# A row ring of twice the size, x loads behind four transposes, index operations behind the low halves, in a routed expert kernel on one core

## The chip, the cores and the metric

One Trainium2 chip, one core of it, one launch. The metric is the device time of the kernel in microseconds (us), lower is better.

## The reference

The input is x of 8 x 3584 tokens with 192 features. A causal filter of 7 taps per head (8 heads of 24 features, taps by a softmax over the weight row) gives 28672 mixed tokens. Each token goes to one of 8 experts:

```
logits = normalize(x) @ normalize(emb).T / tau
e      = argmax(logits);  gate = softmax(logits)[e]
out[t] = gate * (relu(x[t] @ w1[e]) @ w2[e])     # 192 -> 1024 -> 192
```

All of it is float32.

## The kernel before, in words

**Stages.** Tokens are handled in 16 chunks of 1792 (112 partitions x 16). `mix` filters a chunk by matmuls (`conv`, L423) and takes square norms. `route` scales the chunk (`scaled`, L480 and L482) and splits every number into a high and a low float16 half (`rest`, L489 to L495), four groups of four tiles. For each group `turn` (L686) has SP issue a DMA transpose of the rows from SBUF into `xtb`, and `logits` (L676) multiplies it by the embeddings. `rank` picks the expert and counts a place in its list. `put` and `scatter` (L692) have POOL write each token's row, with its number and gate, into the expert's list `rows_d` in DRAM by an indirect DMA, 16 per chunk. `load_x` (L402, L411) loads the x of two chunks later into the buffer that this chunk leaves.

**Experts.** After some chunks `hand_out` opens a phase: each expert gets a block of the next 128 to 512 rows of its list. `fetch` gives SP the loads of one block: two DMA transposes from `rows_d` (L821) into a buffer `e_xT` and one small load `e_mt` (L870) of numbers and gates. Before the change there are three `e_xT` buffers, and `expert` fetches so that the block about to start and the two after it have their loads in SP's queue; a load waits for the scatters that it needs and for its buffer. `block` then runs. For each of its hidden tiles five matmuls go into PSUM (`h_ps`, L940), ACT writes the high halves (relu, L944) and DVE the low halves (L946). Then `gate` has DVE clip the token numbers (`id`, `masked`, L852) and scale the gates (`g`, L915); `id` and `g` have three buffers each. Last come 24 matmuls per 128 rows into `o_ps` (L961), ACT's `y` scaled by `g` (L966), and POOL's indirect DMA of `y` to the rows `id` of the output (L968).

**What sets the order.** SP runs its queue exactly as the program emits it. On PE, ACT, DVE and POOL the framework orders the instructions by a simulated timeline, within the dependences that it knows; an instruction that looks ready there may stand ahead of others that were emitted before it. A dependence without a semaphore only fixes the order on an engine. In `run`, a planner with its own clock (`self.clock`, in us of TensorE work) interleaves pieces of `route`, `mix` and `rank` with the steps of the blocks; logits are emitted at least 7.0 of it after the last transpose (`TURN`). At the end `last_blocks` adds 8 blocks of 512 rows and 20 small ones whose expert is known only at run time; for these, DVE copies the weights into `slot` (L809, L813), the last 6146 columns of the tile `work`. Nothing else uses `slot` after the weights have been prepared.

Of the kernel before, what the change touches and what calls it, by code (L numbers as in the profile page):

```python
# [12 lines left out]
F16 = mybir.dt.float16  # L13
F32 = mybir.dt.float32
# [3 lines left out]
ALU = mybir.AluOpType  # L18
# [4 lines left out]
H = 8  # L23
# [7 lines left out]
NT = 16  # L31
# [12 lines left out]
NFC = F // 128  # L44
# [6 lines left out]
GX = 4  # L51
# [19 lines left out]
AHEAD = 0.4  # L71
OUT = 1.9, 1.6
COST = 14.4, 12.6
WAIT = 0.5, 0.5
# [16 lines left out]
class _Sub:  # L91
    def __init__(self, T, u, need, e=None, c=None, sel=None, j=None):
        self.T, self.u, self.need = T, u, need
        self.e, self.c, self.sel, self.j = e, c, sel, j
        self.xT = self.mt = None


class _Moe:
    def __init__(self, ctx, tc, x, weight, emb, tau, w1, w2, out):
        self.tc, self.nc = tc, tc.nc  # L100
        self.x, self.weight, self.emb, self.tau = x, weight, emb, tau
        self.w1, self.w2, self.out = w1, w2, out
        B, S, _ = x.shape
        self.B, self.S, self.N = B, S, B * S
        self.nch = self.N // CT
        self.per_b = S // CT
        self.cap = self.N + PAD
        self.dummy = E * self.cap
        pool = lambda name, bufs, **k: ctx.enter_context(
            tc.tile_pool(name=name, bufs=bufs, **k))  # L110
        self.cp = pool("const", 1)
        self.xp = pool("xload", 2)
        self.sp = pool("small", 2)
        self.lp = pool("lone", 1)
        self.ep = pool("expert", 3)
        self.yp = pool("y", 3)
        self.op = pool("out", 4)
        self.mp = pool("meta", 6)
        self.hp = pool("phase", 6)
        self.rings = {k: pool("ps_" + k, n, space=PSUM)  # L120
                      for k, n in (("r", 1), ("l", 1), ("h", 6))}

        self.res = self.cp.tile([128, E * RES], F16, name="res")
        self.work = self.cp.tile([128, 2 * NFC * 512 + S2 + RES - W2], F16, name="work")
        self.hid = self.work[:, 0:2 * NFC * 512]
        self.slot = self.work[:, 2 * NFC * 512:]
        self.xtb = self.cp.tile([128, NT // GX, XW], F16, name="xtb")
        self.rows2 = self.cp.tile([TP, 2, NT, SW], I32, name="rows2")
        self.ids = self.cp.tile([TP, NT], I32, name="ids")
        self.xtn = 0  # L130
        self.wexp = self.cp.tile([128, E, 2], I32, name="wexp")
        self.si = self.cp.tile([128, E, 2], I32, name="w_si")
        self.ws = self.cp.tile([128, E, 2], I32, name="w_s")
        self.acc = self.cp.tile([128, E, 2], F32, name="w_acc")
        self.g0 = self.cp.tile([128, E], F32, name="g0")
        self.dp = pool("scratch", 1, space=DRAM)
        self.rows_d = self.dp.tile([E * self.cap + PAD * NJ, RW], I32, name="rows_d")
        self.scatters, self.pend, self.step = [], [], None
        self.nput, self.final = 0, False
        self.vacant = [0.0, 0.0]  # L140
        self.lims, self.pace = {}, 1.0
        self.xts, self.mixed, self.n2 = [], {}, {}
        self.raw = {}
        self.tiles, self.lgs, self.ranks, self.zs = {}, {}, {}, {}
        self.subs, self.ready, self.at, self.copied = [], 0, 0, 0
        self.clock, self.mm = 0.0, None
# [51 lines left out]
    def constants(self):  # L198
        nc, cp = self.nc, self.cp
        nc.gpsimd.memset(self.xtb[:].rearrange(  # L200
            "p h (a k t) -> p (h a) k t", k=4, t=TP)[:, :, 3, 0:HALO], 0.0)
        nc.gpsimd.memset(self.rows2[:, :, :, XD + 2:], 0)
        nc.gpsimd.iota(self.ids, pattern=[[TP, NT]], base=TP - 1,
                       channel_multiplier=-1)
        head = self.ep.tile([128, 4 * 512], F16, tag="xT", name="head")[:].bitcast(F32)
        self.idf, self.onef = head[:, 0:128], head[:, 128:256]
        make_identity(nc, self.idf)
        self.idh = head[:, 256:320].bitcast(F16)
        nc.vector.tensor_copy(out=self.idh, in_=self.idf)
        nc.gpsimd.memset(self.onef, 1.0)  # L210
        self.oneh = cp.tile([128, 128], F16, name="oneh")
        nc.gpsimd.memset(self.oneh, 1.0)

        self.lth = cp.tile([128, 128], F16, name="lth")
        nc.gpsimd.memset(self.lth, 1.0)
        nc.gpsimd.affine_select(
            out=self.lth, in_=self.lth, pattern=[[1, 128]], base=0,
            channel_multiplier=-1, compare_op=ALU.is_gt, fill=0.0)

        tmp = self.op.tile([128, D], F32, tag="y", name="tmp")[:, 0:2 * E + 64].bitcast(I32)  # L220
        e8i = tmp[0:TP, 0:E]
        nc.gpsimd.iota(e8i, pattern=[[-1, E]], base=E, channel_multiplier=0)
        self.e8 = cp.tile([TP, E], F32, name="e8")
        nc.vector.tensor_copy(out=self.e8, in_=e8i)

        self.rst = cp.tile([TP, E, NT], F32, name="rst")
        nc.gpsimd.memset(self.rst, 1.0)
        nc.gpsimd.memset(self.rst[:, :, 0:1], 0.0)

        rn = tmp[:, E:E + NJ]  # L230
        nc.gpsimd.iota(rn, pattern=[[128, NJ]], base=1, channel_multiplier=1)
        self.rn = cp.tile([128, NJ], F32, name="rn")
        nc.vector.tensor_single_scalar(out=self.rn, in_=rn, scalar=float(self.N),
                                       op=ALU.mult)

        cbi = tmp[:, E + 64:]
        nc.gpsimd.iota(cbi, pattern=[[self.cap, E]], base=0, channel_multiplier=0)
        self.cb = cp.tile([128, E], F32, name="cb")
        nc.vector.tensor_copy(out=self.cb, in_=cbi)

        self.start = cp.tile([128, E], F32, name="start")
        nc.vector.tensor_copy(out=self.start, in_=cbi)

    def conv_taps(self, w):
# [10 lines left out]
        nc.vector.tensor_scalar(out=w, in0=w, scalar1=z[:, 0:1], scalar2=None,  # L255
                                op0=ALU.mult)

        seq = self.ep.tile([128, 3 * 512], F16, tag="xT", name="cseq")[
            0:H, :].bitcast(F32)[:, 0:2 * 128]
        nc.vector.memset(seq, 0.0)  # L260
        nc.vector.tensor_copy(out=seq[:, TP + 9:TP + 9 + KT], in_=w)
        sd = self.dp.tile([H, 2 * 128], F32, name="cseq_d")
# [235 lines left out]
    def route(self, c):  # L498
        xTs = []
# [3 lines left out]
        for g in range(NT // GX):  # L503
            self.scaled(c, g)
            yield 0.9, 0.85
            self.rest(c, g)
            yield 0.95, 0.0
            if g < 2:
                xTs.append(self.turn(c, g))
        if c + 2 < self.nch:  # L510
            self.load_x(c + 2)
        for g in range(2, NT // GX):
            xTs.append(self.turn(c, g))
        yield self.clock + TURN
        for g in range(NT // GX):
            self.logits(lg, xTs[g], g)
# [174 lines left out]
    def scatter(self, idx, src):  # L691
# [5 lines left out]
            self.tc.declare_no_dep(i, group=k, reason="rows are distinct")  # L697
        self.tc.add_to_no_dep_group("put", i)
        self.scatters.append(i)


    def pads(self):
# [130 lines left out]
    def first_rows(self, k):  # L833
        nc = self.nc
        if not k:
# [3 lines left out]
                tensor=m.tensor, offset=m.offset,  # L839
                ap=[[RW, 128], [RW * self.cap, E], [1, 2]])).ins], NT)  # L840
            self.x0 = []
        x = self.ep.tile([128, 4 * 512], F16, tag="xT", name="e_xT")
        for i in range(4):
            e = 4 * k + i
            v = x[:, i * 512:(i + 1) * 512].rearrange("p (k t) -> p k t", t=128)
            self.after(self.rows_of(e * self.cap, v, 128, NT), NT)
            self.x0.append(v)

    def masked(self, ids, lim, name):
        n = int(np.prod(ids.shape[1:]))  # L850
        o = self.yp.tile([128, 8], I32, tag="id", name=name)[:, 0:n]
        self.nc.vector.scalar_tensor_tensor(  # L852
            out=o, in0=ids, scalar=float(self.N), in1=lim, op0=ALU.min, op1=ALU.max)
        return o

    def fetch(self):
        nc = self.nc
# [3 lines left out]
        if s.u == 0:  # L861
# [1 line left out]
            self.row = nc.sync.value_load(at, min_val=0, max_val=E * self.cap)  # L863
        row = self.row + s.u if s.u else self.row
        T = s.T
        s.xT = self.ep.tile([128, 4 * 512], F16, tag="xT", name="e_xT")[
            :, 0:4 * T].rearrange("p (k t) -> p k t", t=T)
        lds = self.rows_of(row, s.xT, T, s.need)
        s.mt = self.mp.tile([128, 4, 2], I32, tag="mt", name="e_mt")[:, 0:T // 128]
        lds.append(nc.sync.dma_start(  # L870
# [23 lines left out]

    def expert(self):
        nc = self.nc
        while self.ready < min(self.at + 3, len(self.subs)):
            self.fetch()
        s = self.subs[self.at]
        self.copy_w1(self.at)  # L900
# [7 lines left out]
        def gate():  # L908
            if s.e is None:
                ids.extend(s.mt[:, a, 0:1] for a in range(nj))  # L910
            else:
                a = s.u // 128
                m = self.masked(s.mt[:, :, 0], self.lims[s.c][0][:, s.e, a:a + nj], "id")
                ids.extend(m[:, a:a + 1] for a in range(nj))
            nc.vector.tensor_scalar(  # L915
                out=g[:, 0:nj], in0=s.mt[:, :, 1].bitcast(F32),
# [4 lines left out]
    def block(self, T, e, xT, ids, g, gate=None):  # L921
# [12 lines left out]
        for b in range(0, NFC, m):  # L934
            ps = self.ps("h", [128, m, T], F32, "h_ps")
            for c in range(m):
# [6 lines left out]
            self.mm = mm.ins.name  # L943
            self.step = nc.scalar.activation(  # L944
                out=hh[:, b:b + m, :], in_=ps, func=AF.Relu).ins
            nc.vector.scalar_tensor_tensor(  # L946
                out=hl[:, b:b + m, :], in0=ps, scalar=0.0, in1=hh[:, b:b + m, :],
                op0=ALU.max, op1=ALU.subtract)
            self.dt = 5 * m * T / 2400
            yield self.slack(m * T)  # L950
        if gate:
# [213 lines left out]
```

## Time and profile before

| | us |
|---|---|
| median of 3 runs | 1276.82 (1273.12 to 1283.05) |
| profiled execution | 1275.99 |
| its span, first to last instruction | 1274.0 |

| engine | busy us | share of the span |
|---|---|---|
| PE matmul | 1130.4 | 89% |
| DVE | 668.7 | 52% |
| ACT | 599.7 | 47% |
| POOL | 511.8 | 40% |

The mean granted TensorE clock is 0.96. The DMA queue of SP took 37.7% of the 16 DMA engines' span, that of POOL 14.0%. Busy shares are averages over a head of about 100 us (weights and first chunks), a long middle in which chunks are routed beside the experts, up to about 945 us, and a tail of experts alone. "Idle before, releaser" in the profile names what ended an engine's idle time; a wait for several semaphores is put down to the one that came last.

### The profile page before, as it was taken

Reading aid. Unit: us, or ns where it says so; the run is one execution under the profiler, and the core shown is the slowest. Engines: PE = TensorE matmul, PEld = TensorE weight load, DVE = VectorE, ACT = ScalarE, POOL = GpSimd, SP = SyncE. Lnnn points to the kernel's source line nnn. Section 1 sums busy time; section 2 is a strip of 40 time slices with the busy share of each in tenths; the row PEclk is TensorE's granted clock in tenths of the full one; section 3 lists DMA queues with packets and bytes.
Section 4 is the critical chain, followed back from the end, with each engine's and each line's share of the span. In section 5 each row is a group of like instructions: output and inputs, shape, how many; then the busy total and the mean of one; then the engine's idle time right before and its main releaser. Section 6 shows DMA issues by size and latency. Waiting matters only on the chain. (4 is left out here: it accounts for less than half of the span.)

```text
span 1274.0 us, 29634 instructions
## 1 busy us (share of the span) xinstructions
PE 1130.4 (89%) x11188; PEld 905.9 (71%) x11188; DVE 668.7 (52%) x1939; ACT 599.7 (47%) x1414; POOL 511.8 (40%) x523
## 2 busy tenths in 40 slices
PE   5667998787798999898999989999889999999997
PEld 3466887686677877676667666778668778877776
DVE  5996463574374563736364627554643334445443
ACT  4974454454365365454545445643334433333333
POOL 1336225545355447362625343554742213222222
PEclk8878999998998999899999999999999999999999
DMA  9747547756767839475656655574422212322220
GB/s 259 202 112 201 124 82 178 169 117 132 159 121 171 163 85 220 85 172 105 144 118 135 130 117 98 104 143 80 107 74 57 58 45 55 55 52 51 51 49 24
DMA packets 324777, 146.64 MB, mean 115 GB/s; under 512 B 266590, under 2 KB 315101, under 8 KB 324624
## 3 DMA queue, kind: packets, MB, share of 16 engines
q1 hardware_dynamic: 300960, 93.98, 37.7%
q0 software_dynamic: 23664, 50.68, 14.0%
q8 instruction: 89, 1.46, 0.5%
q14 instruction: 64, 0.52, 0.1%
HBM read 38.35 MB, written 51.05 MB: 70 GB/s over the span
## 5 line engine op out<-in xcount | busy, mean ns | idle before, releaser
L961 PEld LDWEIGHTS <-work 128*128 128x128 f16 x5472 | 462.8, 99 | 83.7 <-DVE work L946 36.8
L940 PE MATMUL h_ps<-e_xT,res 128*128 128x384 f16 (+3 forms) x3520 | 493.9, 295 | 28.4 <-DVE work L946 14.2
L961 PE MATMUL o_ps<-res,work 128*128 128x192 f16 x4992 | 458.5, 249 | 41.7 <-DVE work L946 36.8
L940 PEld LDWEIGHTS <-res 128*128 128x128 f16 x3520 | 308.4, 99 | 185.4 <-issue 45.0
L946 DVE SCALAR_TENSOR_TENSOR work<-h_ps,work 128x384 f16<-128x384 f32 (+1 forms) x536 | 316.7, 605 | 170.0 <-ACT work L944 167.2
L944 ACT ACTIVATE work<-h_ps 128x384 f16<-128x384 f32 (+1 forms) x536 | 283.6, 534 | 247.0 <-PE h_ps L940 229.4
L968 POOL DMA_INDIRECT out_dram<-y,id x208 | 213.8, 1028 | 416.9 <-ACT y L966 370.4
L692 POOL DMA_INDIRECT rows_d<-rows,di x256 | 259.2, 1012 | 172.9 <-issue 64.7
L966 ACT ACTIVATE y<-o_ps,g 128x192 f32<-128x192 f32 x228 | 93.7, 420 | 270.2 <-PE o_ps L961 255.8
L423 PE MATMUL conv_ps<-xt,band 128*112 128x384 f32 x256 | 114.3, 542 | 6.0 <-DMA band<-cseq_d 3.8
L426 ACT COPY xt<-conv_ps 112x384 f32<-112x384 f32 x128 | 61.4, 484 | 82.7 <-PE conv_ps L423 80.3
L915 DVE TENSOR_SCALAR g<-e_mt,res 128x3 f32<-128x3 f32 (+3 forms) x80 | 18.1, 227 | 145.2 <-ACT y L966 106.3
L852 DVE SCALAR_TENSOR_TENSOR id<-e_mt,lim 128x3 int32<-128x3 int32 (+3 forms) x80 | 12.8, 160 | 154.9 <-DMA out_dram<-y,id 79.2
L435 ACT ACTIVATE sq<-xt 112x192 bf16<-112x192 f32 x196 | 70.7, 361 | 4.7
L482 ACT CAST rows<-xt 112x768 f16<-112x768 f32 x64 | 52.6, 833 | 27.5 <-DMA rows_d<-rows,di 16.2
L968 POOL DMA_INDIRECT out_dram<-y,e_mt x20 | 24.3, 1216 | 95.3 <-ACT y L966 95.3
L480 DVE TENSOR_TENSOR xt<-xt,x_p_s 112x768 f32<-112x768 f32 x64 | 58.1, 950 | 0.0
L423 PEld LDWEIGHTS conv_ps<-xt,band 128*112 128x112 f32 x256 | 41.6, 193 | 17.6 <-issue 8.3
L940 PE MATMUL h_ps<-e_xT,work 128*128 128x128 f16 x800 | 49.9, 219 | 4.3 <-DVE work L809 4.3
L940 PEld LDWEIGHTS <-work 128*128 128x128 f16 x800 | 46.6, 98 | 5.2 <-DVE work L809 5.2
L961 PE MATMUL o_ps<-work 128*128 128x192 f16 x480 | 45.9, 246 | 4.2 <-DVE work L813 3.3
L489 DVE TENSOR_TENSOR rows<-xt,rows 112x512 f16<-112x512 f32 x64 | 43.6, 681 | 3.4 <-ACT rows L482 3.4
(165 smaller groups left out, 577.4 us busy)
## 6 DMA issues: line engine op xcount, KB each, us to landing
xt<-in_dram SPq DMA_DIRECT2D x8, 1536.0 KB
xt<-in_dram SPq DMA_DIRECT2D x7, 1440.0 KB
res<-in_dram SPq DMA_DIRECT2D x6, 768.0 KB
rows_d<-rows,di POOLq DMA_INDIRECT x256
e_xT<-rows_d SPq DMA_TRANSPOSE x216
out_dram<-y,id POOLq DMA_INDIRECT x208
res<-in_dram SPq DMA_DIRECT2D x5, 512.0 KB
work<-in_dram SPq DMA_DIRECT2D x3, 512.0 KB
```

The lines of the kernel that those rows point to most:

```text
L423: self.behind(nc.tensor.matmul(out=ps, lhsT=self.band[:, h, :], rhs=xt[:, :, h * G:(h + 1) * G], start=True, stop=True))
L426: nc.scalar.copy(out=xt[0:TP, :, h * G:(h + 1) * G], in_=ps)
L435: nc.scalar.activation(out=sq, in_=xc[:, t, :], func=AF.Square, accum_out=n2[:, t:t + 1])
L480: self.nc.vector.tensor_tensor(out=xc[:, u, :], in0=xc[:, u, :], in1=sb, op=ALU.mult)
L482: self.nc.scalar.copy(out=self.rows2[:, c % 2].bitcast(F16)[:, u, 128:128 + D], in_=xc[:, u, :])
L692: i = self.nc.gpsimd.indirect_dma_start(out=self.rows_d[:, :], out_offset=bass.IndirectOffsetOnAxis(ap=idx, axis=0), in_=src, in_offset=No ...
L940: mm = nc.tensor.matmul(out=ps[:, c, :], lhsT=wa[:, o:o + 128], rhs=xT[:, k, :], start=(i == 0), stop=(i == 4))
L944: self.step = nc.scalar.activation(out=hh[:, b:b + m, :], in_=ps, func=AF.Relu).ins
L946: nc.vector.scalar_tensor_tensor(out=hl[:, b:b + m, :], in0=ps, scalar=0.0, in1=hh[:, b:b + m, :], op0=ALU.max, op1=ALU.subtract)
L961: mm = nc.tensor.matmul(out=o, lhsT=h[:, c, q], rhs=w2[:, c, k:k + D], start=(i == 0), stop=(i == len(parts) - 1))
L966: self.step = nc.scalar.activation(out=y, in_=o, func=AF.Copy, scale=g[:, a:a + 1]).ins
L968: i = nc.gpsimd.indirect_dma_start(out=self.out[:, :], out_offset=bass.IndirectOffsetOnAxis(ap=ids[a], axis=0), in_=y, in_offset=None, bou ...
```

## The change

The pool of three `e_xT` buffers goes. Its bytes become one tile `xr` of 6144 columns, and `slot`, as long as no run-time expert needs it, is its second half. `place` lays blocks one behind the other over both halves (eight blocks of 384 rows fit), over the first alone once the last blocks are planned. `ahead` decides how far to fetch: three blocks are always fetched, as before; up to seven if all their scatters have been emitted and the planner's clock is 6.0 past the last of them (`SETTLE`), and if the place is free of all blocks from the one before the current on. `e_mt` gets eight buffers for six. In `route`, each transpose follows its group's split, and `load_x` comes behind all four. `masked` orders `id` behind the block's last low half on DVE.

```diff
+HALF = 3 * 2048
+SETTLE = 6.0
...
-        self.ep = pool("expert", 3)
-        self.mp = pool("meta", 6)
+        self.mp = pool("meta", 8)
...
+        self.xr = self.cp.tile([128, HALF], F16, name="xr")
+        self.pos, self.puts = 0, []
...
@@ route
             yield 0.95, 0.0
-            if g < 2:
-                xTs.append(self.turn(c, g))
+            xTs.append(self.turn(c, g))
         if c + 2 < self.nch:
             self.load_x(c + 2)
-        for g in range(2, NT // GX):
-            xTs.append(self.turn(c, g))
@@ scatter
         self.scatters.append(i)
+        self.puts.append(self.clock)
@@ masked
-    def masked(self, ids, lim, name):
+    def masked(self, ids, lim, name, behind=None):
...
+        if behind is not None:
+            _dep(self.tc, i, behind, False)
         return o
+
+    def place(self, T):
+        n, p = 4 * T, self.pos
+        if p % HALF + n > HALF:
+            p = (p // HALF + 1) * HALF
+        return 0 if p + n > (HALF if self.final else 2 * HALF) else p
+
+    def ahead(self):
+        if self.ready == len(self.subs):
+            return False
+        if self.ready < self.at + 3:
+            return True
+        if self.ready > self.at + 6:
+            return False
+        s, p = self.subs[self.ready], self.place(self.subs[self.ready].T)
+        if s.need > len(self.puts) or self.clock < self.puts[s.need - 1] + SETTLE:
+            return False
+        return all(v.p >= p + 4 * s.T or p >= v.p + 4 * v.T
+                   for v in self.subs[max(0, self.at - 1):self.ready])
@@ fetch
-        s.xT = self.ep.tile([128, 4 * 512], F16, tag="xT", name="e_xT")[
-            :, 0:4 * T].rearrange("p (k t) -> p k t", t=T)
+        s.p = self.place(T)
+        self.pos = s.p + 4 * T
+        v = self.xr if s.p < HALF else self.work
+        p = s.p if s.p < HALF else s.p - HALF + 2 * NFC * 512
+        s.xT = v[:, p:p + 4 * T].rearrange("p (k t) -> p k t", t=T)
@@ expert
-        while self.ready < min(self.at + 3, len(self.subs)):
+        while self.ahead():
             self.fetch()
...
-                m = self.masked(s.mt[:, :, 0], self.lims[s.c][0][:, s.e, a:a + nj], "id")
+                m = self.masked(s.mt[:, :, 0], self.lims[s.c][0][:, s.e, a:a + nj], "id",
+                                self.last)
@@ block
-            nc.vector.scalar_tensor_tensor(
+            self.last = nc.vector.scalar_tensor_tensor(
                 out=hl[:, b:b + m, :], in0=ps, scalar=0.0, in1=hh[:, b:b + m, :],
-                op0=ALU.max, op1=ALU.subtract)
+                op0=ALU.max, op1=ALU.subtract).ins.name
```

The constants of the head and the rows of the first eight blocks, which lay in the old pool, now lie in `xr`.

## Rows read from the trace of the kernel before

**Rows 1.** Stretches: us, busy us (count) of PE, PEld, DVE, ACT, POOL; clock; DMA.
```profile
400.00:500.00 100.00, 95.01 (x916) 77.05 (x917) 58.10 (x191) 51.68 (x124) 49.36 (x50) 0.98 0.67 141
1000.00:1100.00 100.00, 99.79 (x947) 77.60 (x946) 43.79 (x77) 39.76 (x78) 23.13 (x23) 1.00 0.21 49
```

**Rows 2.** Waits of PE and SP over the run: us in total, times, longest.
```profile
PE o_ps L961 <- DVE work L946: 36.8, 31, 5.1
PE h_ps L940 <- DVE work L946: 14.2, 11, 4.7
PE h_ps L940 <- DMA e_xT<-rows_d: 14.0, 3, 7.5
PE lg_ps L676 <- DMA xtb<-rows: 9.9, 2, 5.7
...
SPq L821 <- PE h_ps L940: 295.1, 55, 14.0
SPq L686 <- DVE rows L495: 91.0, 11, 22.6
```

**Rows 3.** Waits of DVE before id and g, same columns.
```profile
DVE g L915 <- ACT y L966: 111.8, 26, 6.3
DVE id L852 <- DMA out_dram<-y,id: 79.2, 37, 6.5
DVE id L852 <- DMA e_mt<-rows_d: 75.7, 16, 11.7
DVE g L915 <- DMA e_mt<-rows_d: 29.3, 7, 10.8
```

**Rows 4.** Timeline of DVE, 732 to 748 us: start, us, what, idle before.
```profile
739.61 0.16 DVE L852 SCALAR_TENSOR_TENSOR id<-e_mt,lim 128x3 int32<-128x3 int32 x1 [6.49 <-DMA out_dram<-y,id]
739.69 1.48 DVE L946 SCALAR_TENSOR_TENSOR work<-h_ps,work 128x384 f16<-128x384 f32 x3
747.44 0.23 DVE L915 TENSOR_SCALAR g<-e_mt,res 128x3 f32<-128x3 f32 x1 [6.27 <-ACT y L966]
```

**Rows 5.** Timeline of PE, 640 to 916 us.
```profile
640.81 1.86 PE L940 MATMUL h_ps<-e_xT,res 128*128 128x384 f16 x10 [0.48 <-DVE work L946]
...
727.78 6.66 PE L940 MATMUL h_ps<-e_xT,res 128*128 128x384 f16 x40
740.30 6.60 PE L961 MATMUL o_ps<-res,work 128*128 128x192 f16 x55 [3.79 <-DVE work L946]
832.62 6.10 PE L961 MATMUL o_ps<-res,work 128*128 128x192 f16 x72 [0.72 <-DVE work L946]
...
915.44 3.83 PE L961 MATMUL o_ps<-res,work 128*128 128x192 f16 x44 [2.08 <-DVE work L946]
```

**Rows 6.** Timeline of DVE and PE around 402 us.
```profile
401.84 0.16 DVE L852 SCALAR_TENSOR_TENSOR id<-e_mt,lim 128x2 int32<-128x2 int32 x1 [6.70 <-DMA e_mt<-rows_d]
403.07 0.50 PE L961 MATMUL o_ps<-res,work 128*128 128x192 f16 x2 [5.12 <-DVE work L946]
```

**Rows 7.** At 514 us: a PE row, then a stretch, columns as rows 1.
```profile
514.65 3.36 PE L940 MATMUL h_ps<-e_xT,res 128*128 128x384 f16 x10 [4.68 <-DVE work L946]
514.00:518.00 4.00, 3.35 (x12) 1.65 (x12) 4.00 (x15) 1.05 (x5) 0.00 (x0) 0.50 0.00 0
```

**Rows 8.** Timeline of SP's queue, 275 to 298 us, and PE's next row.
```profile
275.77 3.88 SPq L686 DMA_TRANSPOSE xtb<-rows  x2
279.76 1.22 SPq L411 DMA_DIRECT2D xt<-in_dram  x1
281.03 12.59 SPq L686 DMA_TRANSPOSE xtb<-rows  x2
294.78 2.50 SPq L821 DMA_TRANSPOSE e_xT<-rows_d  x2
297.49 0.42 SPq L870 DMA_DIRECT2D e_mt<-rows_d  x1
...
299.03 1.01 PE L940 MATMUL h_ps<-e_xT,res 128*128 128x128 f16 x8 [7.46 <-DMA e_xT<-rows_d]
```

More of the change, by code (lines that the diff above doesn't have):

```diff
@@ L94, in __init__ @@
         self.e, self.c, self.sel, self.j = e, c, sel, j
-        self.xT = self.mt = None
+        self.xT = self.mt = self.p = None
 class _Moe:
@@ L204, in constants @@
                        channel_multiplier=-1)
-        head = self.ep.tile([128, 4 * 512], F16, tag="xT", name="head")[:].bitcast(F32)
+        head = self.xr[:, 0:2048].bitcast(F32)
         self.idf, self.onef = head[:, 0:128], head[:, 128:256]
@@ L256, in conv_taps @@
                                 op0=ALU.mult)
-        seq = self.ep.tile([128, 3 * 512], F16, tag="xT", name="cseq")[
-            0:H, :].bitcast(F32)[:, 0:2 * 128]
+        seq = self.xr[0:H, 2048:2048 + 2 * 256].bitcast(F32)
         nc.vector.memset(seq, 0.0)
@@ L841, in first_rows @@
             self.x0 = []
-        x = self.ep.tile([128, 4 * 512], F16, tag="xT", name="e_xT")
         for i in range(4):
             e = 4 * k + i
-            v = x[:, i * 512:(i + 1) * 512].rearrange("p (k t) -> p k t", t=128)
+            v = self.xr[:, 2048 + e * 512:2048 + (e + 1) * 512].rearrange("p (k t) -> p k t", t=128)
             self.after(self.rows_of(e * self.cap, v, 128, NT), NT)
             self.x0.append(v)
-    def masked(self, ids, lim, name):
+    def masked(self, ids, lim, name, behind=None):
         n = int(np.prod(ids.shape[1:]))
         o = self.yp.tile([128, 8], I32, tag="id", name=name)[:, 0:n]
-        self.nc.vector.scalar_tensor_tensor(
-            out=o, in0=ids, scalar=float(self.N), in1=lim, op0=ALU.min, op1=ALU.max)
-        return o
+        i = self.nc.vector.scalar_tensor_tensor(
+            out=o, in0=ids, scalar=float(self.N), in1=lim, op0=ALU.min, op1=ALU.max).ins
+        if behind is not None:
+            _dep(self.tc, i, behind, False)
+        return o
+    def place(self, T):
[15 more added lines that the diff above has]
+                   for v in self.subs[max(0, self.at - 1):self.ready])
     def fetch(self):
```

## The prediction, made before the result was known

> **What bounds the kernel now.** I read the stretches first. In the tail PE is busy 99.8 of 100 us at full clock; nothing is to be had there. Before 945 us it is not: 95 of 100 us at clock 0.98 in one of the better stretches [rows 1]. So the path is PE, and what can be won is PE's waits in the routed middle. The list of waits, read next, names them [rows 2]: 51.0 us in 42 waits for the low halves of DVE (36.8 and 14.2), 14.0 for `e_xT`, 9.9 for `xtb`. DVE is half idle, so it is not slow there but held. Its own list says by what [rows 3]: `id` waits 79.2 us for an output transfer and 75.7 for `e_mt`, `g` 111.8 for `y` and 29.3 for `e_mt`. Most of that costs nothing. It costs where low halves stand behind it in DVE's order, and the timelines show this: at 739.61 `id` ends a wait of 6.49 for an output transfer, three low halves follow at once, and PE resumes at 740.30 after 3.79 idle [rows 4, 5]. That transfer belongs to an earlier block whose `id` buffer is wanted again: the instruction stands about two blocks too early. At 401.84 the same happens with `e_mt` [rows 6].
>
> **A stall costs twice.** [...] Ten matmuls of 384 columns take 3.36 there [rows 7] and 6.66 / 4 = 1.67 at the upper level [rows 5]: 1.7 lost. After 740.30, 55 matmuls take 6.60 where 6.10 x 55 / 72 = 4.66 is due: 1.9 lost [rows 5]. I count nine such stalls before 945 us and 1.8 each.
>
> **The change part by part.**
>
> *Index operations.* Nothing is added; 80 `id` operations of 0.16 move on DVE. Of the 51.0 us, 11.7 lie in 14 waits, the first at 640.81 and the last at 915.44 [rows 5], in which DVE does work of its own (splits of a chunk, the choice of the last blocks); they stay. Another 3.7 are short waits, or parts of waits, with other DVE work before them. 35.6 follow `id` or `g`. Of these 12.1 are late `e_mt`: 5.12 [rows 6], 4.68 [rows 7], and 2.3 after the longest wait of `g` [rows 3]. The other 23.5 are `id` waiting for an output transfer, and they go: behind its own block's last low half `id` asks for a buffer whose transfer was issued two blocks earlier, some 25 us (two times 6.66 + 6.10 [rows 5]). What is behind the moved `id`: `g` of a later block, the next low halves, and POOL's output transfer, which needs `y` anyway and thus 24 matmuls more. New wait: none expected.
>
> *Ring.* The 80 blocks keep their transposes and small loads. SP's wait for PE to leave a buffer, 295.1 us [rows 2], mostly goes. Loads of a phase whose scatters are done are then up to seven blocks early. That takes the late `e_mt` (12.1) and those `e_xT` waits whose block is not the first of its phase: 6.5 of 14.0. The third wait, 7.46 at 299.03 [rows 8], is a phase's first block; its load is forced, as before, and still comes behind the transposes and now directly behind the x load. It saves perhaps 3.1. So 9.6 of 14.0. Cost: the copies of weights into `slot` must wait for blocks lying there. The first is needed in the tail, behind the first block that the ring lays without `slot`; I take 0, and as a bound the time of one small block, (6.66 + 6.10) / 3 = 4.
>
> *x load.* A pair of transposes takes SP 3.88, but 12.59 behind an x load [rows 8]; I count 12 such pairs, of 8.9 to 12.6. Two of them made PE wait, 9.9 [rows 2]. These go. The x load moves back by the two transposes, some 4 us; no wait of PE for x stands in the list of waits, and a chunk's filter runs a chunk after its load, which covers it. Next late in SP's queue is the row load behind the x load: it takes over the hold of 12.59 - 3.88 = 8.7. For a block of 384 rows fetched two blocks ahead, 25 us cover it; for a phase of 128 rows nothing does, and that is the 7.46 above.
>
> *Clock.* Of nine stalls eight go: 8 x 1.8 = 14.
>
> *Back.* With PE earlier, the splits of a chunk meet low halves more often. The four chunks where this is seen alone cost 2.0 each; I take five more, 10. And some waits of `g` will now stand ahead of low halves. The bounds: 0, as in 747.44, where `g` waited 6.27 and PE did not [rows 4], and the whole 23.5. I take a quarter, 6, as nearly all 26 waits of `g` for `y` [rows 3] were free.
>
> Sum: 23.5 + 12.1 + 9.9 + 9.6 + 14 - 10 - 6 = 53. The profiled execution is 1275.99 (span 1274.0), the median 1276.82, under 0.1% apart: 1276 - 53 = **1223**. Without the give-backs it is 1207; with twice as much, and the 299 us stall whole, 1242.
>
> **A rule weighed against it.** The row shows a load held by the x load that was issued before it [rows 8]. The Trainium skill, DMA: Bandwidth & Descriptors, section "Queues, rings and completion order", says that each DMA engine takes the descriptors of one issuer's row in ring order, so moving the x load only chooses who is held. The trace agrees with the hold of 8.7; it doesn't show row loads in that place. This is the second rival.
>
> **Rivals.**
> 1. *`g` takes the place of `id`.* It is not ordered by the change and has 111.8 us of waits. Against: its wait ends with `y`, without POOL's queue and a transfer after it, at the time when PE turns to the next block. If it comes so, 23.5 and three clock losses (5.4) stay: 53 - 29 = 24, so **1252**.
> 2. *The x load's hold falls on row loads.* Then the 9.9 comes back as waits for `e_xT`, and the 9.6 with two clock losses (3.6) isn't won: 53 - 23 = 30, **1246**. For: one of the three waits is already of this kind. Against: loads of most phases are long in the ring by then.
> 3. *The ring hardly opens* (scatters emitted too late, places taken), so the change doesn't do what it says: 12.1, 9.6 and three clock losses stay, 53 - 27 = 26, **1250**. For: a phase opens only after `rank`, and 16 scatters must be out. Against: eight blocks of 384 rows fill it exactly.
> 4. *Slower: loads fetched ahead stand in front of a chunk's transposes.* Five loads take SP 5 x (2.50 + 0.42) = 14.6 [rows 8], more if one waits for scatters still in POOL's queue. Today a delay of 8.7 costs PE something in 2 chunks of 12. Past some 9 us it decides: 5.9 more in each of 12 chunks, with 1.8 of clock, is 92: 1223 + 92 = **1315**. Against: SP stands 91.0 us waiting for the splits now [rows 2], so it has room, and without its waits for buffers the burst comes earlier.
>
> **How the numbers follow.** Forecast 0.60 (own range 1207 to 1242), rivals 0.10, 0.09 and 0.07, slower 0.06. The other 0.08: all instructions are ordered anew, and new waits elsewhere eat the gain, within 1%, about what a measurement can't tell from no change (1264 to 1290). Rivals 1 to 3 give 1246 to 1252 and count as faster, with a little spilling over: faster 0.84, same 0.10, slower 0.06. The range of 1206 to 1258 holds the forecast and the first three rivals and leaves out under 0.2.
>
> **What would show it.** Right: hardly any wait of `id`; PE's waits for low halves near 15 to 25 us, for `xtb` 0, for `e_xT` under 8; the clock at 1.00 around 515 and 740 us; four transposes, then the x load, in SP's queue; SP's waits for PE a small part of 295. Wrong: DVE's waits of `g` ending together with PE's; PE waiting for `e_xT` right behind x loads; PE waiting for `xtb` with row loads in front of it on SP; a PE order that differs so much that no stretch answers to one of before.

## The result, and the profile after

| | before | after |
|---|---|---|
| median, us | 1279.9 (1273.12 to 1283.05, 4 runs) | 1218.57 (1217.28 to 1221.27, 4 runs) |
| profiled execution, us | 1275.99 | 1219.62 |
| its span, us | 1274.0 | 1217.7 |
| PE busy, us | 1130.4 | 1111.8 |
| mean granted clock of TensorE | 0.960 | 0.971 |

The ratio after to before is 0.953, 95% interval 0.9482 to 0.9578: faster. The runs of before include the three shown earlier. The forecast was 1223, the range 1206 to 1258.

The span fell by 56.3 us. PE's busy time fell by 18.6 and its idle time by 37.7 (143.6 to 105.9), so the whole difference is looked for on PE. The line of busy times, from the page of the changed kernel (busy us, share of the span, instructions):

```profile
PE 1111.8 (91%) x11188; PEld 899.5 (74%) x11188; DVE 678.0 (56%) x1939; ACT 598.0 (49%) x1414; POOL 507.4 (42%) x523
```

The counts are those of the same work; only when it happens changed. The waits of PE, of SP and of DVE in the changed kernel (us in total, times, longest) answer to [rows 2, 3]:

```profile
PE o_ps L985 <- DVE work L970: 14.1, 12, 4.5
PE lg_ps L675 <- DMA xtb<-rows: 12.1, 5, 6.0
PE h_ps L964 <- DMA xr<-rows_d: 11.7, 1, 11.7
...
PE h_ps L964 <- DVE work L970: 5.5, 7, 1.9
...
SPq L821 <- PE h_ps L964: 227.7, 58, 43.3
...
DVE g L939 <- ACT y L990: 170.1, 38, 8.0
...
DVE g L939 <- DMA e_mt<-rows_d: 23.3, 5, 10.0
```

PE's waits for low halves (L970) went from 51.0 us in 42 waits to 19.6 in 19. DVE's two lines of `id`, 154.9 us together, are gone: no `id` waits any more. The waits of `g` for `y` and for `e_mt` grew from 141.1 [rows 3] to 193.4. `xtb` and the rows cost PE about what they did.

The stretches of the changed kernel, columns as rows 1:

```profile
200.00:300.00 100.00, 77.27 (x881) 67.43 (x879) 51.02 (x185) 47.45 (x131) 47.77 (x49) 0.86 0.67 144
...
400.00:500.00 100.00, 99.54 (x949) 79.36 (x947) 62.49 (x209) 55.66 (x148) 51.46 (x54) 1.00 0.77 161
500.00:600.00 100.00, 98.72 (x871) 75.04 (x870) 55.63 (x176) 54.55 (x138) 52.22 (x54) 1.00 0.72 151
```

From 400 to 600 us the middle now looks like the tail: PE is busy 99.54 and 98.72 of 100 us at clock 1.00, where it was 95.01 at 0.98 in the first of them [rows 1]; from 600 to 900 us it is 95.68 to 96.54, also at 1.00. The largest piece that is left to win behind the head lies between 200 and 300 us, where PE is idle 22.7 us, and two places of SP's queue are most of it. The timeline of SP's queue in the changed kernel (start, us, what):

```profile
234.88 2.50 SPq L821 DMA_TRANSPOSE work<-rows_d  x2
237.63 0.37 SPq L893 DMA_DIRECT2D e_mt<-rows_d  x1
238.18 12.38 SPq L685 DMA_TRANSPOSE xtb<-rows  x4
...
270.87 11.81 SPq L685 DMA_TRANSPOSE xtb<-rows  x4
282.73 0.57 SPq L413 DMA_DIRECT2D xt<-in_dram  x1
284.52 6.29 SPq L821 DMA_TRANSPOSE xr<-rows_d  x2
291.02 0.42 SPq L893 DMA_DIRECT2D e_mt<-rows_d  x1
292.19 2.48 SPq L821 DMA_TRANSPOSE xr<-rows_d  x2
```

The same stretch on PE:

```profile
243.22 0.22 PE L675 MATMUL lg_ps<-ma,xtb 128*128 128x16 f16 x2 [5.98 <-DMA xtb<-rows]
...
251.04 0.21 PE L675 MATMUL lg_ps<-ma,xtb 128*128 128x16 f16 x2 [1.80 <-DMA xtb<-rows]
...
295.58 2.72 PE L964 MATMUL h_ps<-xr,res 128*128 128x128 f16 x24 [11.68 <-DMA xr<-rows_d]
```

Six blocks' loads, 3.9 us apart and without a break from 214.04 on, end at 238.00, and only then do a chunk's four transposes follow; PE waits 5.98 and 1.80 us for them. At 282.73 the x load stands behind the four transposes as intended, and the next row load takes 6.29 where its like takes 2.48. PE waits 11.68 for it; in [rows 8] it waited 7.46 for that block. The data did not come later: up to the row at 295.58 PE has run as many matmuls into `h_ps` and `o_ps` (960 and 768) as up to 299.03 before, so they came 3.45 us earlier. But PE was ready for them 7.67 earlier, at 283.90 instead of 291.57. In the first 296 us the changed kernel has thus won 3.45 of its 56.3 us.

### The profile page after: what moved, and what is told of

The parts are those of the page before. It is cut to its first block, busy times and chain, and to the rows that moved or that the text cites. A ratio compares the mean times of both kernels' runs of the same rounds, so it can differ in the third digit from the quotient of the medians.

```text
span 1217.7 us, 29732 instructions
## 1 busy us (share of the span) xinstructions
PE 1111.8 (91%) x11188; PEld 899.5 (74%) x11188; DVE 678.0 (56%) x1939; ACT 598.0 (49%) x1414; POOL 507.4 (42%) x523
## 3 DMA queue, kind: packets, MB, share of 16 engines
q0 software_dynamic: 23664, 50.68, 14.5%
## 4 chain that ended last, share of the span: by engine, by line
PE 68%; DVE 11%; DMA 7%; issue 5%; ACT 4%; POOL 2%; SPq 1%; DVEq 0%; POOLq 0%; ACTq 0%
PE h_ps L964 31%; PE o_ps L985 31%; PE conv_ps L425 6%; ACT sq L437 2%; DVE xt L482 2%; POOL rows_d L691 2%; DMA rows_d<-rows,di 2%; DVE work L970 2%; DVE res L385 1%; DMA xtb<-rows 1%; DVE rows L491 1%; DMA xr<-rows_d 1%; DVE work L813 1%; SPq L821 1%; DVE rows L494 1%
## 5 line engine op out<-in xcount | busy, mean ns | idle before, releaser
L985 PE MATMUL o_ps<-res,work 128*128 128x192 f16 x4992 | 449.3, 247 | 15.5 <-DVE work L970 14.1
L970 DVE SCALAR_TENSOR_TENSOR work<-h_ps,work 128x384 f16<-128x384 f32 (+1 forms) x536 | 322.6, 606 | 224.2 <-ACT work L968 221.3
L964 PE MATMUL h_ps<-xr,res 128*128 128x384 f16 (+3 forms) x2240 | 317.5, 298 | 13.7 <-DMA xr<-rows_d 11.7
L691 POOL DMA_INDIRECT rows_d<-rows,di x256 | 254.9, 996 | 147.1 <-issue 48.2
L964 PE MATMUL h_ps<-work,res 128*128 128x384 f16 (+2 forms) x1280 | 173.2, 289 | 3.8 <-DVE work L970 3.7
L425 PE MATMUL conv_ps<-xt,band 128*112 128x384 f32 x256 | 108.5, 517 | 8.3 <-DMA band<-cseq_d 4.7
L964 PE MATMUL h_ps<-xr,work 128*128 128x128 f16 x800 | 49.9, 219 | 0.0
```

What stands on the lines that cost most here:

```text
L425: self.behind(nc.tensor.matmul(out=ps, lhsT=self.band[:, h, :], rhs=xt[:, :, h * G:(h + 1) * G], start=True, stop=True))
L691: i = self.nc.gpsimd.indirect_dma_start(out=self.rows_d[:, :], out_offset=bass.IndirectOffsetOnAxis(ap=idx, axis=0), in_=src, in_offset=No ...
L964: mm = nc.tensor.matmul(out=ps[:, c, :], lhsT=wa[:, o:o + 128], rhs=xT[:, k, :], start=(i == 0), stop=(i == 4))
L970: self.last = nc.vector.scalar_tensor_tensor(out=hl[:, b:b + m, :], in0=ps, scalar=0.0, in1=hh[:, b:b + m, :], op0=ALU.max, op1=ALU.subtra ...
L985: mm = nc.tensor.matmul(out=o, lhsT=h[:, c, q], rhs=w2[:, c, k:k + D], start=(i == 0), stop=(i == len(parts) - 1))
```

## The experiments

The runs came in four groups, each on a chip of its own; which chip the first measurement ran on is not on record. In the first, second and fourth group the kernel before took 1333 to 1344 us; in the third it took 1278.5, as in the first measurement (1279.9). A ratio is therefore compared with ratios of its own group, or between the third group and the first measurement, whose times before agree. "A slower chip" below stands for a group of the first kind; each chip was used once, so chip and hour can't be told apart.

### One part left out, or one part alone

`no_id`: the changed kernel, `id` not ordered.

```diff
-                m = self.masked(s.mt[:, :, 0], self.lims[s.c][0][:, s.e, a:a + nj], "id",
-                                self.last)
+                m = self.masked(s.mt[:, :, 0], self.lims[s.c][0][:, s.e, a:a + nj], "id")
```

> All of the change but the order of id. Theory A (id ahead of the low halves was the main loss; the ring only brings e_mt early): the waits of id for output transfers come back, PE's waits for low halves rise from 19.6 us to about 19.6 + 23.5 = 43, with some clock, 1245 to 1252 us. Theory B (SP's waits for buffers were the main loss, and the ring cured them): PE's waits for low halves stay near 20 us and the time near 1220 to 1228.

`no_turns`: the changed kernel, two of the four transposes behind the x load as before.

```diff
-            xTs.append(self.turn(c, g))
+            if g < 2:
+                xTs.append(self.turn(c, g))
...
+        for g in range(2, NT // GX):
+            xTs.append(self.turn(c, g))
```

> All of the change but the x load behind four transposes. In the changed kernel PE still waits 12.1 us for xtb, now behind row loads. Theory A as forecast (the order is worth 9.9 us and some clock): 1228 to 1235, PE's waits for xtb 20 us or more. Theory C (SP's burst of row loads, not the x load, now holds the transposes): within 5 us of 1218.6 either way, the waits for xtb 10 to 15.

`no_ring`: the changed kernel with the three `e_xT` buffers and the three blocks of before (the main lines of the edit against the changed kernel).

```diff
-        while self.ahead():
+        while self.ready < min(self.at + 3, len(self.subs)):
             self.fetch()
...
-        s.p = self.place(T)
-        self.pos = s.p + 4 * T
...
+        s.xT = self.ep.tile([128, 4 * 512], F16, tag="xT", name="e_xT")[
+            :, 0:4 * T].rearrange("p (k t) -> p k t", t=T)
```

> The kernel before with the order of id and the four transposes, without ring. Theory A: id's waits are gone either way, late e_mt now holds only g; PE's waits for low halves 20 to 32 us, for e_xT 14 or more as the x load now stands before row loads; 1232 to 1240. Theory B: most of the gain is lost, 1255 or more.

`id_only`: the kernel before, with the order of `id` alone.

```diff
+        if behind is not None:
+            _dep(self.tc, i, behind, False)
...
-                m = self.masked(s.mt[:, :, 0], self.lims[s.c][0][:, s.e, a:a + nj], "id")
+                m = self.masked(s.mt[:, :, 0], self.lims[s.c][0][:, s.e, a:a + nj], "id",
+                                self.last)
```

> The kernel before with the order of id alone. Theory A: 23.5 us of waits go, those behind late e_mt on id too (5 of 12.1), three or four clock losses of 1.8; PE's waits for low halves fall from 51.0 to 20 to 28; 1237 to 1248. Theory B (SP's buffer waits): 1265 or more. Rival 1 of the prediction (g takes id's place): waits for low halves stay above 40, 1265 or more.

Measured beside the kernel before (1343.04 us median of 20 runs): `no_id` 1344.99, ratio 1.0022 (0.9997 to 1.0047); `no_turns` 1336.34, 0.9945 (0.9918 to 0.9971); `no_ring` 1327.36, 0.9874 (0.9838 to 0.991); `id_only` 1332.41, 0.9906 (0.987 to 0.9942).

Without the order of `id` nothing is gained; with it alone something is, as its interval lies below 1. The waits of PE for low halves point the same way, 32.2 us in `no_id` and 25.2 in `id_only`, but they are no proof by themselves: `ring_only`, below, has 23.7 without the order. All sizes are well below those of the first measurement. The times expected above were given for a kernel before of 1277 us and can't be held against these runs, and the whole change had no time on a slower chip, so it was run again.

### The changed kernel again, and the other parts alone

`after_again`: the changed kernel, no edit.

> The changed kernel once more, to stand beside its parts on one chip. The kernels without one part were timed in a session where the kernel before took 1343 us, 5% more than in the runs shown first, and PE stood for some 60 us with nothing that the profile shows in front of it. Theory A (parts add, each removes its own waits of PE): 0.953 to 0.975 of the kernel before. Theory D (what held PE there is not touched by the change and takes over as the bound): 0.98 to 1.00.

`ring_only`: `no_id` and `no_turns` together, so that only the ring is left of the change.

> The ring alone: x loads between the transposes and id free in DVE's order, as before. Theory A: it takes the late e_mt (12 us) and two of three waits for e_xT (6.5), and puts row loads before the transposes; the waits of id for output transfers stay near 79 us: 0.98 to 0.99 of the kernel before. Theory B (SP's buffer waits were the main loss): 0.965 or less.

`turns_only`: the kernel before, with four transposes ahead of the x load.

```diff
-            if g < 2:
-                xTs.append(self.turn(c, g))
+            xTs.append(self.turn(c, g))
...
-        for g in range(2, NT // GX):
-            xTs.append(self.turn(c, g))
```

> The x load behind four transposes alone. Theory A: the 9.9 us that PE waits for xtb and two clock losses go, the x load now stands before row loads of which three blocks at most are fetched: waits for e_xT rise from 14 to 18 to 25: 0.992 to 1.000. If the hold only moves: 0.998 to 1.003.

`one_more`: the changed kernel, at most one load beyond the three fetched per block.

```diff
-        while self.ahead():
+        n = 0
+        while self.ahead() and (self.ready < self.at + 3 or n < 1):
+            n += self.ready >= self.at + 3
             self.fetch()
```

> The changed kernel, but at each block at most one load beyond the three is fetched, so that SP's bursts of row loads in front of transposes are shorter. Theory C (bursts hold the transposes: six loads, 24 us, ahead of those on which PE waited 6.0): PE's waits for xtb fall from 12.1 to under 5, 3 to 10 us faster than the changed kernel. If the bursts cost nothing: within 3 us of it.

Measured beside the kernel before (1333.23 us, 19 runs): `after_again` 1319.56, ratio 0.9869 (0.9812 to 0.9926); `ring_only` 1340.23, 1.0028 (0.9994 to 1.0062); `turns_only` 1332.96, 0.998 (0.9947 to 1.0014); `one_more` 1318.05, 0.9885 (0.9823 to 0.9948).

The same program that took 1218.57 us takes 1319.56 here, and the change is worth 1.3% instead of 4.7%: the span of theory D, not of theory A. The waits of PE in `after_again` show where the difference sits (us in total, times, longest):

```profile
PE o_ps L985 <- issue: 39.1, 48, 6.8
PE h_ps L964 <- issue: 23.7, 36, 3.1
PE o_ps L985 <- DVE work L970: 11.2, 14, 2.4
```

"issue" is time in which an engine waited for nothing that the profile shows. In the changed kernel's first profile PE has no such line. The timeline of PE in `after_again` shows what it looks like:

```profile
944.33 0.32 PE L985 MATMUL o_ps<-res,work 128*128 128x192 f16 x1 [0.92 <-issue]
945.06 0.33 PE L985 MATMUL o_ps<-res,work 128*128 128x192 f16 x1 [0.41 <-issue]
947.15 0.32 PE L985 MATMUL o_ps<-res,work 128*128 128x192 f16 x1 [1.77 <-issue]
948.55 0.32 PE L985 MATMUL o_ps<-res,work 128*128 128x192 f16 x1 [1.08 <-issue]
```

Matmuls for which the profile shows nothing to wait for, and which elsewhere stand close behind one another, come one at a time, and starts are 0.7, 1.4 or 2.1 us apart. PE is idle 74.5 us in "issue" and, at the lower clock, busy 44.2 more (1156.0 against 1111.8), with 14.5 less of other idle time: together the 104.2 us between the two spans. PE's waits for rows are gone and those for `xtb` are 2.9; loads have more time where PE is slower, which would explain it, but no run shows that this is the reason. `ring_only` and `turns_only` gain nothing here, as `no_id` gained nothing; for `ring_only` neither theory had this. In the four groups every kernel with the order of `id` is faster than the kernel before, by its interval, and none of the three without it is. `one_more` has no wait for `xtb` at all, but its ratio can't be told from that of the changed kernel, and with 2.9 us of such waits there was little to win on this chip: what the bursts cost stays open.

### Two of them on a chip like the first

`id_only_2` and `no_ring_2` are `id_only` and `no_ring` once more.

> The order of id alone, a second time. On the two chips so far all engines stood for times with nothing in front of them (PE some 70 us of it), the kernel before took 1333 to 1343 us, and id alone gave 0.991, the whole change 0.987. If the chip is like them: 0.988 to 0.994 again. If it is like the runs shown first (kernel before near 1277 us): theory A, id is the largest part, waits of PE for low halves fall from 51 to 20 to 28 us, 0.966 to 0.978. Rival 1 of the prediction (g takes its place): 0.99 or more.

> Order of id and four transposes, no ring, a second time; with the run beside it and the whole change it splits the gain in three steps: id, then transposes, then ring. If the chip is like the last two: 0.985 to 0.990. If it is like the runs shown first: theory A has the transposes worth 0.005 to 0.012 and the ring 0.005 to 0.015, so 0.962 to 0.972; theory B (the ring freed SP and that was the main gain): 0.975 or more, with the ring worth over 0.02.

Measured beside the kernel before (1278.52 us, 7 runs): `id_only_2` 1243.01, ratio 0.9729 (0.9667 to 0.9791); `no_ring_2` 1246.44, 0.9762 (0.97 to 0.9825). With 0.953 (0.9482 to 0.9578) for the whole change, the order of `id` is worth some 35 us, the order of the transposes after it nothing that can be told from zero, and the ring after both some 28 (1246.44 to 1218.57 in the first measurement; the two intervals do not touch). These sizes hold for the parts in this sequence: the ring, or the transposes, without the order of `id` were run on a slower chip only. `id_only_2` lies in the span of its theory A (0.966 to 0.978). The 2.3% of the ring are more than the 0.5 to 1.5% that theory A gave it, and on the side of theory B.

The waits of PE and DVE in `id_only_2` (the profile is of a run of 1250.27, the slowest of its four):

```profile
PE o_ps L964 <- DVE work L949: 21.2, 18, 6.2
PE lg_ps L676 <- DMA xtb<-rows: 11.9, 2, 7.5
...
PE h_ps L943 <- DVE work L949: 9.9, 8, 4.1
PE h_ps L943 <- DMA e_xT<-rows_d: 9.2, 3, 6.2
...
PE o_ps L964 <- DVE id L852: 6.4, 1, 6.4
...
DVE g L918 <- DMA e_mt<-rows_d: 114.9, 19, 11.2
DVE g L918 <- ACT y L969: 107.8, 24, 6.3
```

By the profile's names the waits for low halves fall from 51.0 to 31.1. The 6.4 put down to `id` is one more of them. The timeline of DVE, and then PE's row:

```profile
399.28 0.23 DVE L918 TENSOR_SCALAR g<-e_mt,res 128x2 f32<-128x2 f32 x1 [8.07 <-DMA e_mt<-rows_d]
...
399.69 0.68 DVE L949 SCALAR_TENSOR_TENSOR work<-h_ps,work 128x512 f16<-128x512 f32 x1
400.30 0.15 DVE L852 SCALAR_TENSOR_TENSOR id<-e_mt,lim 128x2 int32<-128x2 int32 x1
...
400.44 0.50 PE L964 MATMUL o_ps<-res,work 128*128 128x192 f16 x2 [6.44 <-DVE id L852]
```

`g` waits for a late `e_mt` with the low half behind it, as `id` did at 401.84 in [rows 6]; `id` itself waits for nothing. So 37.5 us are left, more than the 20 to 28 expected. The order of `id` takes away what `id` waits for output transfers, but not a late `e_mt`: that wait moves from `id` to `g`, 29.3 [rows 3] to 114.9. The three longest waits of PE behind it, 6.44, 6.18 and 4.14, are 16.8 of the 37.5.

The waits of PE, SP and DVE in `no_ring_2`, where SP has the four transposes first:

```profile
PE o_ps L961 <- DVE work L946: 21.9, 18, 9.1
PE h_ps L940 <- DMA e_xT<-rows_d: 20.3, 4, 8.5
PE h_ps L940 <- DVE work L946: 13.6, 11, 4.5
PE o_ps L961 <- ACT work L944: 10.0, 3, 7.3
...
SPq L818 <- PE h_ps L940: 297.8, 53, 12.4
...
DVE g L915 <- DMA e_mt<-rows_d: 164.9, 25, 12.9
```

No wait for `xtb` is left, and the waits for rows rise from 9.2 in `id_only_2` to 20.3. The timeline of SP's queue in `no_ring_2`, with PE's row last, shows the exchange:

```profile
271.50 10.64 SPq L683 DMA_TRANSPOSE xtb<-rows  x4
282.20 1.03 SPq L411 DMA_DIRECT2D xt<-in_dram  x1
284.90 5.12 SPq L818 DMA_TRANSPOSE e_xT<-rows_d  x2
...
291.50 2.49 SPq L818 DMA_TRANSPOSE e_xT<-rows_d  x2
...
294.73 2.72 PE L940 MATMUL h_ps<-e_xT,res 128*128 128x128 f16 x24 [8.47 <-DMA e_xT<-rows_d]
```

That is the second rival at work: the x load's hold falls on row loads, and PE waits for them. The Trainium skill, DMA: Bandwidth & Descriptors, section "Queues, rings and completion order", says that each DMA engine takes the descriptors of one issuer's row in ring order; this trace agrees with it, by 5.12 us behind the x load against 2.49 for the next pair.

What the ring then does is read from `no_ring_2` against the changed kernel: `g` waits 23.3 us for `e_mt` instead of 164.9, and PE's waits for low halves fall from 35.5 to 19.6 (those right behind a `g` that waited for `e_mt`, from 18.4 to 6.6), those for rows from 20.3 to 11.7 and those for ACT's high halves from 10.0 to 1.1, while 12.1 for `xtb` come back.

### What the ring's gain hangs on

`no_turns_2` is `no_turns` once more. `room_only3` is the changed kernel with the room of the ring, but three blocks fetched at most.

> The changed kernel with two of a chunk's four transposes back behind the x load. Theory A (the ring is worth its 2.3% by itself, and the order of the transposes is worth nothing): ratio to the kernel before 0.950 to 0.962, PE's waits for xtb 5 to 12 us and for the rows 0 to 10, together not over 20. Theory B (the ring pays only because all four transposes stand ahead of the x load: otherwise the loads fetched ahead and the x load both hold two of the transposes): ratio 0.968 to 0.980, PE's waits for xtb over 20 us.

```diff
-        if self.ready > self.at + 6:
+        if self.ready > self.at + 2:
```

> The changed kernel with the room of the ring, but never more than three blocks fetched. Theory A (what the ring gives is the early fetch of rows, numbers and gates): ratio to the kernel before 0.970 to 0.980, as the kernel without the ring had (0.976), and g's waits for e_mt on DVE stay near 165 us. Theory B (what it gives is that a load no longer waits in SP's queue for a buffer that PE holds): ratio 0.950 to 0.960, SP's waits for PE's h_ps far below 298 us and g's waits for e_mt below 60.

Measured beside the kernel before (1344.01 us, 19 runs): `no_turns_2` 1336.08, ratio 0.9953 (0.9917 to 0.9989); `room_only3` 1331.42, 0.9907 (0.9873 to 0.9941). It was a slower chip again, and neither theory's ratio came, so the question is not settled in time. `no_turns_2` repeats `no_turns` (0.9945): the ring with two transposes behind the x load gains less than the whole change did on another such chip (0.9869, 0.9812 to 0.9926), and less than `id_only` there (0.9906), though these intervals touch. Its trace has 6.6 us of waits for `xtb` and 5.6 for rows, in the span of theory A; so if the transposes pay beside the ring, it is not by the waits that theory B named. In `room_only3` SP waits 211.5 us for PE's `h_ps` and `g` waits 43.4 for `e_mt`, the signs of theory B; but `g` stays below 60 without the ring too on a slower chip (58.6 in `no_ring`), so that they decide little. `after_again` has 10.1: of the gain in `e_mt` the larger part, 43.4 to 10.1, came with the early fetch, on chips where it is worth little. No run took less time than the changed kernel in the first measurement.

## Why the prediction was right

The total was right: 53 was forecast from the profiled execution, 56.4 came (1275.99 to 1219.62). The main mechanism was right too, but two terms failed, a third came half, the give-backs did not come, and the clock's term came by another count than the forecast's. The errors cancel, so the closeness of 53 and 56 is in part luck. Term by term, in us of PE:

| term | forecast | measured | from |
|---|---|---|---|
| `id` waiting for output transfers | 23.5 | 23.5 | `id` waits nowhere any more |
| late `e_mt` | 12.1 | 5.5 | 2.03 at 220.26 and 4.53 at 336.70 are left |
| `xtb` | 9.9 | -2.2 | 9.9 to 12.1 |
| rows | 9.6 | 2.3 | 14.0 to 11.7 |
| clock | 14 | 18.6 | all of PE's busy time, 1130.4 to 1111.8 |
| chunk splits and `g` | -16 | 2.4 | short waits 3.7 to 0.7, DVE's own work 11.7 to 12.3, `g` for `y` 0 |
| all other waits of PE | 0 | 6.2 | the rest of 56.3 |
| sum | 53 | 56.3 | |

**Index operations: right.** The place that the forecast read is clean now. The timeline of DVE in the changed kernel, 335 to 751 us, and a row of PE:

```profile
335.82 0.23 DVE L939 TENSOR_SCALAR g<-e_mt,res 128x2 f32<-128x2 f32 x1 [9.62 <-DMA e_mt<-rows_d]
335.96 1.28 DVE L970 SCALAR_TENSOR_TENSOR work<-h_ps,work 128x512 f16<-128x512 f32 x2
337.16 0.15 DVE L851 SCALAR_TENSOR_TENSOR id<-e_mt,lim 128x1 int32<-128x1 int32 x1
...
705.24 0.23 DVE L939 TENSOR_SCALAR g<-e_mt,res 128x3 f32<-128x3 f32 x1 [5.98 <-ACT y L990]
713.54 0.15 DVE L851 SCALAR_TENSOR_TENSOR id<-e_mt,lim 128x3 int32<-128x3 int32 x1
...
336.70 1.30 PE L985 MATMUL o_ps<-res,work 128*128 128x192 f16 x9 [4.53 <-DVE work L970]
```

At 713.54 `id` starts without a wait, behind its block's low halves; at 739.61 it had waited 6.49 in front of them [rows 4]. By itself this is confirmed by `id_only_2`, where `id` has no wait either. It gains 51.0 - 37.5 = 13.5 us of waits for low halves and not 23.5, because more late `e_mt` falls on `g`. The 23.5 was not quite `id` alone: the 3.39 at 580.63 had 3.6 us of a chunk's scaling (L480) between `id` and the low halves, and 1.28 of it is left at 552.40, counted under chunk splits; before the 2.79 at 941.68 `g` waited 3.86 for ACT. The first rival, `g` in the place of `id`, is in the first row above in small, for `e_mt`: `g` waits 9.62 for `e_mt`, the low halves stand behind it, and PE resumes 4.53 late at 336.70. Its waits for `y`, 170.1 us in 38 waits, stand before none of PE's waits for low halves; the quarter that the forecast took for them was too much.

**Ring: right that it makes `e_mt` early, wrong on the rows.** `no_ring_2` against the changed kernel shows 15.9 less waiting for low halves, of which the late `e_mt` explains 18.4 - 6.6 = 11.8. That the copies into `slot` cost nothing was right: PE's waits for them are 3.3 us as before (L813), and the 4.3 for L809 are gone. But the one wait for rows that is left is the first block of a phase, 11.68 at 295.58; the forecast had this block saving 3.1 of its 7.46, and it lost 4.2. This step failed outright. The load did come some 3 us earlier, as forecast; but the forecast took this off the wait as if PE would come when it came before, and PE came 7.67 earlier. The second rival adds to it in this place: "its load is forced, as before, and still comes behind the transposes and now directly behind the x load" was seen, and the 6.29 against 2.48 that it costs was not priced. Also wrong: SP's waits for PE did not become a small part of 295.1, they are 227.7. That SP fills the ring and then waits for the next place, as it waited for the next buffer, fits the 58 waits but was not tested.

**x load: wrong.** The two waits of before for `xtb` are gone and five others came, 12.1 in all. Those at 243.22 and 251.04 are the fourth rival in small: loads fetched ahead stand in front of a chunk's transposes. It was given a point from which it decides, some 9 us of delay; one burst passed it, six loads in a row that take SP 24 us, and cost 5.98 and 1.80 there. The forecast counted 2.92 us for a load; with the gaps between them they are 3.9 apart. The other two of size, 1.95 at 167.29 and 2.13 at 349.12, look the same in SP's queue: the chunk's last transpose (163.07 and 342.21) stands directly behind five and three row loads. So it happened in three chunks and not in each of 12, 12.1 us in all, and the kernel is not slower. `no_ring_2`, which fetches three blocks at most, has no wait for `xtb`. Two of the signs that the forecast named for "wrong" came in these places: PE waiting for rows behind an x load, and for `xtb` behind row loads.

**Clock: the size came, the count did not.** The stretch from 514 us that was at 0.50 [rows 7], in the changed kernel (columns as rows 1; the work there is not the same any more):

```profile
514.00:518.00 4.00, 4.00 (x33) 2.81 (x31) 1.34 (x3) 1.81 (x4) 3.00 (x4) 1.00 1.02 181
```

The forecast counted nine stalls and took eight to go at 1.8 each; no run shows that. In the kernel before, the nine longest waits of PE from 200 to 945 us are 3.11 to 7.46; in the 2 us after them the granted clock is 0.50 six times (the lower of its two levels, 1.2 of 2.4 GHz), 0.79 and 0.63 once each, and 1.00 after the one at 615.89, so that one of the nine lost no clock. In the changed kernel three such waits are left, 5.98 at 243.22, 11.68 at 295.58 and 4.53 at 336.70, with 0.50, 0.50 and 0.59 behind them. Six went and not eight, which at 1.8 would give 10.8. The mean granted clock rose from 0.960 to 0.971; an estimate from that alone is 1130.4 x (1 - 0.960 / 0.971) = 12.8. So the 18.6 is PE's busy time for the same instructions, and not all of it is shown to be the clock.

**Give-backs: wrong.** Chunk splits meet low halves at the chunks where they did before, for 12.3 us instead of 11.7, not at five more. So 26.0 were missing in `e_mt`, `xtb` and rows, and 29.2 more than forecast came from PE's busy time (4.6), the give-backs (18.4) and the other waits (6.2).

## What to carry to other kernels

A waiting instruction costs what is queued behind it on its engine: look for the one that stands too early in an in-order queue, and put it behind the work that the bound engine needs; here the place of 80 operations of 0.16 us was worth 35 us. Then look at what comes to stand there instead: here `g`, with the late `e_mt`. Moving a large transfer in a queue only chooses who is held, so ask who comes next and how much slack that one has. A wait is the time between two arrivals: when the bound engine comes earlier, a transfer that comes only a little earlier costs more than before. And a buffer that lets an engine run ahead needs a rule for what it must not run ahead of. When a program's runs differ by chip, compare ratios of one chip, and look first at whether the waits that the change removes are there at all.

## What the runs showed of the hardware that was not expected

The same program, with the same instructions, took 1218.57 us in the first measurement and 1319.56 in the second group, and the kernel before 1279.9 and, on one more chip, 1278.52, against 1333.23 to 1344.01 on three chips. On the slower ones PE stands idle in "issue" for 56.6 to 74.5 us in every profile taken there, DVE too (`after_again`: 69.7 us before low halves), and the granted clock of the profiled runs is lower (0.934 to 0.950 against 0.957 to 0.971). The work of one instruction is not longer: the 192-column matmuls of 400 to 900 us take 245 ns on average in the changed kernel and 247 in `after_again`. In the tail there are stretches without any such loss: from 1000 to 1100 us of `after_again` PE is busy 100.00 of 100 at clock 1.00. A bad stretch of the same run, 938 to 954 us, has PE busy 4.99 of 16.00 us at clock 0.54:

```profile
938.00:954.00 16.00, 4.99 (x23) 2.25 (x23) 2.22 (x3) 0.42 (x1) 10.39 (x12) 0.54 0.27 85
```

What the engines wait for in "issue" is not in the profile, and no run here tells it; it stays open.
